# Moving early pooling and gate work between GpSimd, ScalarE and VectorE, and two products ahead, in a pooled-attention and mixture-of-experts kernel

## The chip, the cores and the metric

The kernel runs on one core of one Trainium2 chip. The metric is the time of one execution on the device in microseconds (us). A core has a matrix engine (TensorE, PE in the profile; its weight loads are listed as PEld) and three engines for elementwise work: VectorE (DVE), ScalarE (ACT) and GpSimd (POOL). The DMA issues named here come from SyncE (SP) or GpSimd. PE and its accumulators meet in PSUM; everything else is in SBUF. Each engine runs its instructions in the order in which the kernel issues them to it.

## The reference

All tensors are float32. An attention over keys and values that are averaged in groups of eight is followed by a mixture of experts in which each token goes to one expert:

```python
B, H, S, D = 8, 8, 576, 64            # q, k, v
k_p = k.reshape(B, H, 72, 8, D).mean(axis=3)
v_p = v.reshape(B, H, 72, 8, D).mean(axis=3)
scores = scale * q @ k_p.T            # 576 x 72 for each batch and head
attn = exp(scores - max); attn /= sum(attn) + 1e-9
x = (attn @ v_p) laid out as 4608 tokens x 512

N, D, E, F = 4608, 512, 8, 1024
logits = x @ w_gate + modality_bias[modality_id]
e_idx = argmax(logits); gate = softmax(logits)[e_idx]
out[token] = gate * (relu(x @ w1[e_idx]) @ w2[e_idx])
```

The inputs q, k and w_gate are drawn eight times as large as their base draw, so that the softmax is not flat.

## The kernel before, in words

**Stages.** The attention with its routing fills about the first 170 us; the products of the expert stage (lines 193, 196, 1314 of the profile) take most of the rest. The change lies in the attention.

**Tiles and steps.** A tile is 128 tokens with all eight heads. A batch of 576 tokens has four tiles of 128 and 64 tokens over; the 64 tokens of two batches make one mixed tile. So a pair of batches has nine tiles, and `steps` lists five steps for it: two tiles, two tiles, the mixed tile, two tiles, two tiles. There are 20 steps. Steps 0 and 1 are batch 0 (tiles 0 to 3), step 2 is mixed tile 4, which needs the keys and values of batches 0 and 1, steps 3 and 4 are batch 1 (tiles 5 to 8), step 5 is the first of batch 2. Each step handles its heads in two halves, written (n,0) and (n,1).

**What a step does.** The helpers are named after their engine:

- `q_pe`/`q_act` (L555, L561): PE transposes the queries into a PSUM slot, ScalarE copies them out to `qt`.
- `s_pe` (L574 mixed, L580): the scores, from `qt` and the keys `kt`. `s_dve` (L587, L590) takes the row maximum and subtracts it; `s_act` (L602, L603) takes the exponent.
- `t_pe`/`t_act` (L609, L614) transpose a tile's weights and copy them to `pt`; `t4_pe`/`t4_act` (L621, L628) do it for the eight pooled keys of every head beyond the first 64.
- `a_pe` (L644, L648): the tile's products with the values, into the one `av` buffer of PSUM. `x_dve` (L667 to L677) divides by the sums and writes the tokens to `xb`; it is what frees `av` for the next tile.

**Keys and values.** The keys of a batch come as four chunks of 128 partitions x 512 elements and a smaller one. Averaging folds the 512 elements to 64. `fold` does it on GpSimd with three adds (L330 to L332), `reduce8` on VectorE with one reduction (L335). In `pool_k` and `pool_v`, conditions on the batch number choose who folds which chunk; `pool_k_rest` and `pool_v_rest` fold one chunk (number 3) later, on VectorE. `kp` has one buffer, `vp` two. `k_operand` (PE transposes, then two ScalarE copies, L383 and L384, to `kt`) runs in two parts, for chunks 0 to 2 and for the rest. `v_operand` copies the folded values with masks to `vw` and `v4` and transposes them for the gate (pv, L422 and L423; the copy out of PSUM to `vt`, L427 and L428). `v_gate` multiplies them by `w_gate` on PE, so that the logits come out of the same products as the tokens. The gate product lands in a corner of a score bank, three blocks wide. ScalarE writes two of them with masks to `vw`; the third goes by a ScalarE copy `vg4` (L444) and a GpSimd product with the mask `m4b` (L445) to `v4`.

**PSUM slots.** q_pe, k_operand, v_operand and t_pe share two slots of the tag `tr`; the scores have two buffers, `av` has one.

**Order.** All order is written by hand. The main loop runs over the steps n; in it the helpers stand in one sequence, and lists of functions (`hook_0` to `hook_3`, `hook_q`) add the work for the next batches at five places. For the steps that matter here they hold:

- step 1: `hook_0` pool_v(1), pool_k(2); `hook_q` k_operand(1, 0); `hook_2` pool_v_rest(1), k_operand(1, 1)
- step 2: `hook_1` v_operand(1); `hook_2` v_gate(1)
- step 3: `hook_0` pool_v(2); `hook_1` k_operand(2, 0); `hook_2` pool_v_rest(2); `hook_q` k_operand(2, 1)
- step 4: `hook_0` pool_k(3); `hook_1` v_operand(2); `hook_2` v_gate(2)

In step n the tiles of step n-1 are finished: `old[0]` behind `hook_1`, `old[1]` near the end, behind `hook_2`. In the lines below, `old` is that pair, and `has`, `nxt` tell whether step n and step n+1 exist:

```python
            run(hook_1, n)
            if old:
                a_pe(old[0])
            if has:
                s_dve(n, 1)
```

**Routing.** When both batches of a pair are through, their routing operations (L726 to L786, nearly all on VectorE) go into a list `drip`, from which `gap()` takes operations between the others. The first group is worked off in steps 6 and 7, 62 to 73 us.

**Loads.** SP issues the loads in an order of their own, by step (`step_loads`). In step 0 it issues k(2), the rest of k(2), v(2), its rest, and k(3); in step 1 q(2), v(3), the rest of k(3), the modality numbers and k(4). A whole k, v or q of a batch is 1 MB.

Of the kernel before, what the change touches and what calls it, by code (L numbers as in the profile page):

```python
# [9 lines left out]
F32 = mybir.dt.float32  # L10
# [5 lines left out]
ALU = mybir.AluOpType  # L16
# [6 lines left out]
P = 128  # L23
# [10 lines left out]
def kernel(  # L34
# [12 lines left out]
    nc = tc.nc  # L47
    ctx.enter_context(tc.manual_schedule(engines=ENGINES))
    B, H, S, HD = q.shape
    NTOK, D = out.shape  # L50
    E, _, FF = w1.shape
    POOL = 8
    SPL = S // POOL
    NPAIR = H // 2
# [163 lines left out]
    with ExitStack() as actx:  # L218
        ap = actx.enter_context(tc.tile_pool(name="ap", bufs=1))
# [5 lines left out]
        kraw, k4raw, vraw, v4raw, qpure, qmix = {}, {}, {}, {}, {}, {}  # L225
# [100 lines left out]
        kps, vps, vts = {}, {}, {}  # L326

        def fold(t, out):

            nc.gpsimd.tensor_add(t[..., 0:256], t[..., 0:256], t[..., 256:512])  # L330
            nc.gpsimd.tensor_add(t[..., 0:128], t[..., 0:128], t[..., 128:256])
            nc.gpsimd.tensor_add(out, t[..., 0:64], t[..., 64:128])  # L332

        def reduce8(t, out):
            nc.vector.tensor_reduce(out, t.rearrange("p (u d) -> p d u", u=POOL), axis=AX.X, op=ALU.add)  # L335
# [4 lines left out]
        def pool_k(b, parts=(0, 1)):  # L340
            if b not in kps:
                kps[b] = (ap.tile([P, NCH, HD], F32, tag="kp", bufs=1, name=f"kp_{b}"),
                          ap.tile([64, HD], F32, tag="kp4", bufs=1, name=f"kp4_{b}"))
            kp, kp4 = kps[b]
            t, t4 = kraw[b], k4raw[b]
            for i in parts:
                cs = K_PART[i]
                if b == 0:
                    for c in cs:
                        reduce8(t[:, c, :], kp[:, c, :])  # L350
                    if i == 1:
                        reduce8(t4, kp4)
                else:
                    for c in range(cs[0], cs[-1] + 1, 2):
                        m = min(c + 2, cs[-1] + 1)
                        if b == 1 and c == 2:
                            reduce8(t[:, c, :], kp[:, c, :])
                        elif b > 1 or c < 2:
                            fold(t[:, c:m], kp[:, c:m])
                    if i == 1:  # L360
                        fold(t4, kp4)
# [24 lines left out]
        def pool_v(b):  # L386
            vp = ap.tile([P, NPAIR, HD], F32, tag="vp", bufs=2, name=f"vp_{b}")
            vp4 = ap.tile([P, HD], F32, tag="vp4", bufs=2, name=f"vp4_{b}")
            t, t4 = vraw[b], v4raw[b]
            if b == 0:  # L390
                fold(t4, vp4)
            fold(t[:, 0:2], vp[:, 0:2])
            if b > 2:
                fold(t[:, 2:4], vp[:, 2:4])
            elif b:
                fold(t[:, 2], vp[:, 2])
            else:
                fold(t[:, 2], vp[:, 2])
                reduce8(t[:, 3, :], vp[:, 3, :])
            if b:  # L400
                fold(t4, vp4)
            vps[b] = (vp, vp4)

        def pool_k_rest(b):
            reduce8(kraw[b][:, 3, :], kps[b][0][:, 3, :])

        def pool_v_rest(b):
            reduce8(vraw[b][:, 3, :], vps[b][0][:, 3, :])

        m4b = m_4.rearrange("p (j o) -> p j o", o=1)  # L410

# [18 lines left out]
        def v_gate(b):  # L430
            vt, vt4 = vts[b]
            dw, d4 = vw[b % NB], v4[b % NB]
            if b:
                pg = spare[1][:, 1, 4 * SPL:4 * SPL + 12 * E].rearrange("p (u x) -> p u x", u=3)
            else:
                pg = ps_tr.tile([P, 3, 4 * E], F32, tag="tr", name=f"pg_{b}")
            for u in range(2):
                nc.tensor.matmul(pg[:, u, :], vt[:, u, :], wgb[:, u].rearrange("p g x -> p (g x)"), start=True, stop=True)
            nc.tensor.matmul(pg[:, 2, :], vt4, wg[0:64, 1::2, :], start=True, stop=True)
            pgv = pg[:, 0:2, :].rearrange("p u (g a e) -> p (u g) a e", g=2, a=2)  # L440
            nc.scalar.activation(dw[:, :, 0, HD:HD + E], pgv[:, :, 0, :], AF.Copy, scale=m_a)
            nc.scalar.activation(dw[:, :, 1, HD:HD + E], pgv[:, :, 1, :], AF.Copy, scale=m_b)
            vg4 = ap.tile([P, NPAIR, E], F32, tag="vg4", bufs=1, name=f"vg4_{b}")
            nc.scalar.copy(vg4, pg[:, 2, :].rearrange("p (j e) -> p j e", j=NPAIR))  # L444
            nc.gpsimd.tensor_tensor(d4[:, :, HD:HD + E], vg4, m4b.to_broadcast([P, NPAIR, E]), op=ALU.mult)  # L445


        bias_all = ap.tile([P, NT, E], F32, name="bias_all")
# [74 lines left out]
        def gap(n=2):  # L523

            for _ in range(n):
                if drip and drip[0] not in held:
                    drip.pop(0)()
# [31 lines left out]
        def q_act(n, w):  # L559
            pq = pqs.pop((n, w))  # L560
            nc.scalar.copy(qts[n, w][:, 0:2 * len(steps[n][2]), :], pq)  # L561
# [21 lines left out]
        def s_dve(n, w):  # L583
            nh = 2 * len(steps[n][2])
            scv = scs.pop((n, w))[:, :, 0:nh * SPL].rearrange("p u (h s) -> p u h s", s=SPL)
            mx = ap.tile([P, 2, 4], F32, tag="mx", bufs=2, name=f"mx_{n}_{w}")[:, :, 0:nh]
            nc.vector.reduce_max(mx, scv, axis=AX.X)  # L587
            gap()
            sb = ap.tile([P, 2, 4 * SPL], F32, tag="sb", bufs=2, name=f"sb_{n}_{w}")
            nc.vector.tensor_tensor(sb[:, :, 0:nh * SPL].rearrange("p u (h s) -> p u h s", s=SPL), scv,  # L590
                                    mx.rearrange("p u (h o) -> p u h o", o=1).to_broadcast([P, 2, nh, SPL]), op=ALU.subtract)
            scs[n, w] = sb
# [19 lines left out]
        def t_act(t):  # L612
            pt = ap.tile([P, NPAIR, P], F32, tag="pt", bufs=2, name=f"pt_{t}")
            nc.scalar.copy(pt, pts[t])  # L614
            pts[t] = pt
# [265 lines left out]
        for g in range(len(GROUPS) - 1):  # L881
            n = s1_of[2 * g + 1] + 2
# [65 lines left out]
        def run(hook, n):  # L948
            for fn in hook.get(n, ()):
                fn()  # L950
# [6 lines left out]
        for n in range(N + 1):  # L957
            has, nxt, nxt2 = n < N, n + 1 < N, n + 2 < N
            old = steps[n - 1][2] if n else ()
            two = len(old) > 1  # L960
            ahead = two and has and steps[n][1] is None
            loads(n)
            run(hook_0, n)
            if old:
                t_pe(old[0])
                t_act(old[0])
                if has:
                    s_act(n, 0)
            if has:
                s_pe(n, 1)  # L970
            if due:
                release()
            if old:
                t4_pe(n - 1)
                t4_act(n - 1)
            if n == N:
                run(hook_3, N - 1)
            if ahead:
                t_pe(old[1])
                t_act(old[1])  # L980
            run(hook_1, n)
            if old:
                a_pe(old[0])
            if has:
                s_dve(n, 1)
            if n == 1:
                pool_k_rest(1)
            finish()
            if n == 0:
                q_pe(1, 0)  # L990
                q_act(1, 0)
                v_operand(0)
            if two and not ahead:
                t_pe(old[1])
                t_act(old[1])
            if n == 1 or n == 2:
                q_pe(n + 1, 0)
                q_act(n + 1, 0)
            if nxt:
                q_pe(n + 1, 1)  # L1000
            run(hook_q, n)
            if old:
                x_dve(old[0])
            gap(2)
            if nxt and n:
                q_act(n + 1, 1)
            if has:
                s_act(n, 1)
            if n == 0:
                q_act(n + 1, 1)  # L1010
            if nxt:
                s_pe(n + 1, 0)
            if nxt2 and n > 1:
                q_pe(n + 2, 0)
                q_act(n + 2, 0)
            if nxt:
                s_dve(n + 1, 0)
            if n == 0:
                v_gate(0)
                pool_k(1)  # L1020
            run(hook_2, n)
            finish()
            due = bool(drip) and drip[0] in held
            if two:
                a_pe(old[1])
            if two:
                x_dve(old[1])
            gap(2)
            if n != N - 1:
                run(hook_3, n)  # L1030
            finish()
# [13 lines left out]
    op = [[ps_op.tile([P, 512], F32, name=f"op{i}_{z}") for z in range(2)] for i in range(2)]  # L1045
# [533 lines left out]
```

## Time and profile before

| | |
|---|---|
| time, median of 3 runs | 593.8 us (593.5 to 594.74) |
| the profiled execution | 596.24 us, of which span 594.5 us |
| granted TensorE clock | 0.999 |
| PE busy | 574.1 us, 97% of the span |
| PE weight loads | 499.5 us, 84% |
| DVE busy | 371.9 us, 63% |
| ACT busy | 275.1 us, 46% |
| POOL busy | 192.0 us, 32% |
| DMA | 92.60 MB, mean 156 GB/s |

The span is the time from the first to the last instruction of the profiled execution; the time of that execution has 1.74 us around it. The shares are averages over the whole span, and the stages differ: GpSimd is busy 32% on average, but 60% to over 90% of each of the first eight of the page's 40 equal slices of the span, 119 us, in which it folds keys and values. In lists of instructions, each row has the start in us, the length in us, the engine, the line, the operation, output and input, the tile's shape and the count of like instructions in a row; in brackets stands the idle time of the engine before it and what ended it.

### The profile page before, as it was taken

How to read it: one execution, taken by the hardware profiler on the slowest of the kernel's cores; microseconds unless marked ns; L12 is line 12 of the kernel's file. 1: busy time of each engine (PE TensorE's matmuls, PEld its weight loads, DVE VectorE, ACT ScalarE, POOL GpSimd, SP SyncE). 2: the span in 40 equal slices, each digit the busy share in tenths (PEclk: the TensorE clock that was granted, in tenths of full speed). 3: DMA queues.
4: the chain of work that ended last, by engine and by line, in shares of the span. 5: the costliest groups of instructions: out<-in, count | busy, mean ns of one | idle time of the engine just before them, and what ended most of it. 6: DMA issues, size and time to landing. Idle time of an engine off the chain costs nothing.

```text
span 594.5 us, 12358 instructions
## 1 busy us (share of the span) xinstructions
PE 574.1 (97%) x3539; PEld 499.5 (84%) x3539; DVE 371.9 (63%) x941; ACT 275.1 (46%) x653; POOL 192.0 (32%) x300
## 2 busy tenths in 40 slices
PE   5899999999999999999999999999999999999995
PEld 4789889888898888888888888888888888888994
DVE  5757888789966775566555457855455487465311
ACT  2657667788552233334333337533333474334210
POOL 6689987755000142112102203212102203202101
PEclk9999999999999999999999999999999999999999
DMA  8999979995311752232232377232335742332001
GB/s 247 288 333 265 352 236 309 308 292 177 110 56 39 262 189 85 94 104 92 101 96 92 106 231 233 91 105 92 106 93 179 238 153 79 115 103 87 37 2 55
DMA packets 83426, 92.60 MB, mean 156 GB/s; under 512 B 17871, under 2 KB 58319, under 8 KB 83344
## 3 DMA queue, kind: packets, MB, share of 16 engines
q1 hardware_dynamic: 77424, 72.24, 39.0%
q0 software_dynamic: 5920, 19.44, 9.9%
q8 instruction: 30, 0.49, 0.3%
q14 instruction: 52, 0.43, 0.2%
HBM read 123.06 MB, written 27.58 MB: 253 GB/s over the span
## 4 chain that ended last, share of the span: by engine, by line
PE 78%; DVE 9%; DMA 8%; ACT 2%; issue 1%; POOL 1%; SPq 1%; POOLq 0%; DVEq 0%; ACTq 0%
PE op L1314 32%; PE hp L193 19%; PE hp L196 10%; DMA k<-in_k_dram 5%; PE av L644 4%; PE hp L183 3%; PE sc L580 2%; PE av L648 2%; PE ph L183 1%; PE pp L609 1%; DMA mod<-in_moe_modality_id_dram 1%; DMA xs<-xb 1%; DVE mx L587 1%; DMA out_dram<-obw,slw 1%; PE pq L555 1%
## 5 line engine op out<-in xcount | busy, mean ns | idle before, releaser
L1314 PE MATMUL op<-hl,hh 128*128 128x512 f32 x512 | 161.1, 396 | 0.0
L193 PE MATMUL hp<-xhl,hl 128*128 128x512 f32 x512 | 137.1, 389 | 0.0
L1290 POOL DMA_INDIRECT out_dram<-ob,sidx x34 | 36.6, 1075 | 263.6 <-DVEq L1319 178.6
L193 PEld LDWEIGHTS hp<-xhl,hl 128*128 128x128 f32 x512 | 96.0, 188 | 20.6
L198 ACT COPY ht<-hp 128x256 f32<-128x256 f32 x128 | 47.8, 373 | 130.8 <-PE hp L196 129.8
L199 DVE TENSOR_TENSOR ht<-ht,hp 128x256 f32<-128x256 f32 x128 | 53.7, 419 | 85.7 <-ACT ht L198 84.2
L1314 PE MATMUL op<-hl,hlo 128*128 128x512 f32 x256 | 99.8, 390 | 0.0
L1314 PEld LDWEIGHTS op<-hl,hh 128*128 128x128 f32 x512 | 88.0, 190 | 11.3
L202 DVE SCALAR_TENSOR_TENSOR hlo<-ht,hh 128x256 fp32r<-128x256 f32 x128 | 55.1, 431 | 55.6 <-ACTq L1319 45.4
L196 PEld LDWEIGHTS hp<-xhl,hl 128*128 128x128 f32 x512 | 78.3, 189 | 10.1
L200 ACT ACTIVATE hh<-ht 128x256 fp32r<-128x256 f32 x128 | 53.7, 420 | 67.5 <-DVE ht L199 67.5
L196 PE MATMUL hp<-xhl,hl 128*128 128x256 f32 x512 | 81.3, 281 | 0.0
L1314 PEld LDWEIGHTS op<-hl,hlo 128*128 128x128 f32 x256 | 48.1, 188 | 11.2 <-DVE hlo L202 0.3
L644 PE MATMUL av<-vw,pt 128*128 128x146 f32 (+1 forms) x320 | 49.5, 293 | 1.7 <-DVE xb L677 1.6
L144 POOL DMA_INDIRECT xg<-xs,gidx x36 | 38.6, 1073 | 31.6 <-DVE sidx L815 16.4
L644 PEld LDWEIGHTS av<-vw,pt 128*128 128x128 f32 (+1 forms) x320 | 39.7, 180 | 3.8 <-DVE xb L677 1.4
L580 PE MATMUL sc<-kt,qt 128*128 128x144 f32 x256 | 37.4, 289 | 1.2 <-ACT qt L561 1.0
L580 PEld LDWEIGHTS sc<-kt,qt 128*128 128x128 f32 x256 | 33.1, 190 | 2.2 <-ACT qt L561 0.9
L587 DVE TENSOR_REDUCE mx<-sc 128x8 f32<-128x576 f32 (+1 forms) x40 | 27.6, 691 | 8.1 <-PE sc L580 6.0
L648 PE MATMUL av<-vw,pt 128*128 128x146 f32 (+1 forms) x160 | 30.6, 289 | 0.2 <-POOL vw L445 0.2
L590 DVE TENSOR_TENSOR sb<-sc,mx 128x576 f32<-128x576 f32 (+1 forms) x40 | 27.7, 692 | 2.4 <-DVE mx L587 0.5
L141 DVE TENSOR_TENSOR hl<-raw,hl 128x1024 fp32r<-128x1024 f32 x24 | 29.0, 1217 | 0.0
(277 smaller groups left out, 825.5 us busy)
## 6 DMA issues: line engine op xcount, KB each, us to landing
raw<-in_moe_w_dram SPq DMA_DIRECT2D x288, 256.0 KB
xs<-xb SPq DMA_DIRECT2D x16, 528.0 KB
scr<-xg SPq DMA_DIRECT2D x29, 256.0 KB
k<-in_k_dram SPq DMA_DIRECT2D x7, 1024.0 KB
v<-in_v_dram SPq DMA_DIRECT2D x7, 1024.0 KB
q<-in_q_dram SPq DMA_DIRECT2D x7, 1024.0 KB
y<-scr SPq DMA_DIRECT2D x108, 64.0 KB
v<-in_v_dram SPq DMA_DIRECT2D x16, 128.0 KB
```

Of the source, the lines that this page charges most:

```text
L144: nc.gpsimd.indirect_dma_start(out=x, out_offset=None, in_=xs[0:rows, :], in_offset=IndirectOffsetOnAxis(idx[:, col:col + 1].bitcast(U32), 0),
L193: nc.tensor.matmul(ph, hl[f][:, 0, d * P:(d + 1) * P], ab[:, d, :, 0:SLOT], start=(d == 0), stop=False)
L196: nc.tensor.matmul(ph[:, 0:SLOT], hl[f][:, 1, d * P:(d + 1) * P], ab[:, d, 0, 0:SLOT], start=False, stop=(d == ND - 1))
L198: nc.scalar.copy(t, ph[:, SLOT:2 * SLOT])
L199: nc.vector.tensor_add(t, t, ph[:, 0:SLOT])
L200: nc.scalar.activation(hh, t, AF.Relu)
L202: nc.vector.scalar_tensor_tensor(hlo, t, 0.0, hh.bitcast(F32), op0=ALU.max, op1=ALU.subtract)
L580: nc.tensor.matmul(dst, qt[:, i, :], kt[b % NB][:, :, h * SPL:(h + 1) * SPL], start=True, stop=True)
L644: nc.tensor.matmul(av[hs, u, 2 * VC * gg:2 * VC * (gg + 1)], pt[:, c, hs], vw[y][:, c].rearrange("p a x -> p (a x)"), start=(gg == 0), sto ...
L648: nc.tensor.matmul(dst4[hs], pt4[:, hs], v4[y][:, 2 * u:2 * u + 2, :], start=False, stop=True)
L1290: nc.gpsimd.indirect_dma_start(out=out[:, :], out_offset=IndirectOffsetOnAxis(idx.bitcast(U32), 0), in_=ob, in_offset=None, bounds_check=N ...
L1314: nc.tensor.matmul(ot, l[:, ts_], hl[f][:, w, D:2 * D], start=(f == 0 and n == 0), stop=(f == NF - 1 and n == 2))
```

## The change

- **Folds.** Chunks 2 and 3 of the keys of batch 2 and chunk 2 of the values of batch 1 are no longer folded by GpSimd (three chunks). VectorE does them: the value chunk and the last chunk of k(1) in step 1 behind `s_act(1,1)`, the chunks of k(2) in step 2 behind `s_act(2,1)` and behind `s_dve(3,0)`. The fold of the last chunk of k(1) stood ahead of the x_dve of tile 0 before and stands behind it now.
- **Products ahead.** In step 1 the products and the x_dve of tile 1 go ahead of the first scores of the mixed step (`s_pe(2,0)`); they stood behind `hook_2`. In step 2 the products of tile 2 go ahead of `hook_1`, that is of v_operand(1).
- **Gate product.** In `v_gate`, for every batch, the third block is multiplied by the mask by VectorE, straight out of PSUM into `v4`; the ScalarE copy and the buffer `vg4` are gone, and so is the GpSimd product.

```diff
@@ pool_k
                         if b == 1 and c == 2:
                             reduce8(t[:, c, :], kp[:, c, :])
-                        elif b > 1 or c < 2:
+                        elif b > 2 or c < 2:
                             fold(t[:, c:m], kp[:, c:m])
@@ pool_v
             if b > 2:
                 fold(t[:, 2:4], vp[:, 2:4])
-            elif b:
+            elif b == 2:
                 fold(t[:, 2], vp[:, 2])
-            else:
+            elif b == 0:
                 fold(t[:, 2], vp[:, 2])
                 reduce8(t[:, 3, :], vp[:, 3, :])
...
-        def pool_k_rest(b):
-            reduce8(kraw[b][:, 3, :], kps[b][0][:, 3, :])
-
-        def pool_v_rest(b):
-            reduce8(vraw[b][:, 3, :], vps[b][0][:, 3, :])
+        def pool_k_rest(b, c=3):
+            reduce8(kraw[b][:, c, :], kps[b][0][:, c, :])
+
+        def pool_v_rest(b, c=3):
+            reduce8(vraw[b][:, c, :], vps[b][0][:, c, :])
@@ v_gate
-            vg4 = ap.tile([P, NPAIR, E], F32, tag="vg4", bufs=1, name=f"vg4_{b}")
-            nc.scalar.copy(vg4, pg[:, 2, :].rearrange("p (j e) -> p j e", j=NPAIR))
-            nc.gpsimd.tensor_tensor(d4[:, :, HD:HD + E], vg4, m4b.to_broadcast([P, NPAIR, E]), op=ALU.mult)
+            nc.vector.tensor_tensor(d4[:, :, HD:HD + E], pg[:, 2, :].rearrange("p (j e) -> p j e", j=NPAIR),
+                                    m4b.to_broadcast([P, NPAIR, E]), op=ALU.mult)
@@ main loop
+            if n == 2:
+                a_pe(old[0])
             run(hook_1, n)
-            if old:
+            if old and n != 2:
                 a_pe(old[0])
             if has:
                 s_dve(n, 1)
-            if n == 1:
-                pool_k_rest(1)
...
+            if n == 1:
+                pool_k_rest(1)
+                pool_v_rest(1, 2)
+                a_pe(old[1])
+                x_dve(old[1])
+            if n == 2:
+                pool_k_rest(2, 2)
             if nxt:
                 s_pe(n + 1, 0)
...
             if nxt:
                 s_dve(n + 1, 0)
+            if n == 2:
+                pool_k_rest(2)
...
             run(hook_2, n)
...
-            if two:
+            if two and n != 1:
                 a_pe(old[1])
-            if two:
                 x_dve(old[1])
```

## The prediction

> **What bounds the kernel now.** I read the page's busy shares first, then the windows, then who TensorE (PE) waits for, then the timelines of the attention stage, engine by engine. The page and the windows (columns: busy us with instruction counts of PE, PEld, DVE, ACT, POOL; granted clock; DMA share; GB/s) show where PE is not full:
>
> ```profile
> PE 574.1 (97%) x3539; PEld 499.5 (84%) x3539; DVE 371.9 (63%) x941; ACT 275.1 (46%) x653; POOL 192.0 (32%) x300
> 20.00:30.00 10.00, 8.88 (x66) 7.26 (x65) 7.92 (x16) 6.12 (x18) 7.69 (x12) 1.00 1.08 306
> 40.00:45.00 5.00, 4.83 (x46) 3.88 (x45) 3.29 (x9) 2.76 (x9) 4.68 (x9) 1.00 1.09 356
> 50.00:62.00 12.00, 12.00 (x100) 11.64 (x99) 8.61 (x23) 7.65 (x21) 11.14 (x20) 1.00 1.06 342
> 62.00:73.00 11.00, 10.03 (x82) 8.46 (x81) 10.01 (x31) 8.37 (x26) 10.04 (x20) 1.00 1.06 341
> 170.00:580.00 410.00, 409.94 (x2183) 351.60 (x2182) 235.31 (x574) 160.50 (x348) 76.55 (x77) 1.00 0.36 117
> ```
>
> From 170 to 580 us PE idles 0.06 us: a microsecond won or lost before 170 reaches the end unchanged. So the question is what PE waits for in steps 1 to 4 of the attention loop (20 to 50 us), where the diff moves work, and whether what is won there lasts. The waits of PE, 20 to 80 us (total, times, longest):
>
> ```profile
> PE av L644 <- DVE xb L677: 0.9, 2, 0.6
> PE sc L574 <- ACT kt L384: 0.7, 1, 0.7
> PE pv L422 <- DVE vp L335: 0.5, 1, 0.5
> PE pv L423 <- POOL vp L332: 0.4, 1, 0.4
> PE av L648 <- POOL vw L445: 0.2, 1, 0.2
> ```
>
> The last four lie between 25 and 49 us and the change touches three of them; the first lies in the first routing group (68 to 73 us). PE's timeline there (start, length, x count, idle before), and last a row of VectorE's:
>
> ```profile
> 25.80 0.46 PE L574 MATMUL sc<-kt,qt 128*64 128x144 f32 x2
> 26.92 0.70 PE L574 MATMUL sc<-kt,qt 128*64 128x144 f32 x6 [0.66 <-ACT kt L384]
> 27.96 0.77 PE L644 MATMUL av<-vw,pt 128*128 128x146 f32 x4
> 29.56 0.60 PE L609 MATMUL pp<-ident,pe 128*128 128x128 f32 x4
> 32.12 0.30 PE L423 MATMUL pv<-ident,vp 128*64 128x128 f32 x1 [0.41 <-POOL vp L332]
> 33.76 1.04 PE L555 MATMUL pq<-ident,q 128*128 128x128 f32 x8
> 42.08 0.34 PE L648 MATMUL av<-vw,pt 128*64 128x146 f32 x1 [0.17 <-POOL vw L445]
> 23.83 1.04 DVE L335 TENSOR_REDUCE kp<-k 128x64 f32<-128x512 f32 x1
> ```
>
> **The change, part by part.**
>
> *Tile 1's products (a_pe(1)) ahead of the mixed step's scores.* They take 27.96 to 29.56 = 1.60 us. Placed at 25.80 they fill the wait for ScalarE's key copy, which ends the idle at 26.92: about 0.9 us regained. They need the av buffer free of x_dve(0); the fold of k(1)'s last chunk, which stood ahead of x_dve(0) and takes 1.04 us (last row above), now stands behind it, so VectorE (DVE) reads av sooner and I charge nothing; were it late all the same, the price is at most that 1.04. The cover then lacks elsewhere (estimates from laying the rows out in the new order): the last key chunk's copies, hidden by those products before, now hold s_pe(2,1) some 0.2 us, and s_dve(2,0), queued behind x_dve(1), holds the small transpose L621 another 0.2.
>
> *Tile 2's products ahead of v_operand(1).* They cover POOL's last v4 fold, wait 0.41 us. The transposes pv then stand directly before q_pe(3,1), which needs their PSUM slot: 0.2 us back.
>
> *Three chunk folds from POOL to DVE.* The prices:
>
> ```profile
> 30.40 0.73 POOL L330 TENSOR_TENSOR v<-v 128x256 f32<-128x256 f32 x1
> 31.75 0.32 POOL L332 TENSOR_TENSOR vp<-v 128x64 f32<-128x64 f32 x1
> 28.60 1.05 DVE L335 TENSOR_REDUCE vp<-v 128x64 f32<-128x512 f32 x1
> 33.96 0.17 DVE L667 TENSOR_SCALAR r<-av 128x8 f32<-128x8 f32 x1 [1.95 <-PE av L648]
> ```
>
> One chunk is 1.67 us on POOL (30.40 to 32.07, three adds) and 1.05 on DVE: POOL loses 5.0 us, DVE gains 3.2, all before 38 us. There DVE idles between tiles, 1.95 us ahead of the x_dve at 33.96, and the fold of k(2) stands ahead of scores that come later than its data. I cost the DVE part at nothing; without that cover it is 1.05 us each. No DMA, SP or POOL issue is moved past another; POOL's later folds only come forward.
>
> *The gate product on DVE, eight times.*
>
> ```profile
> L444 ACT COPY vg<-sc x7: 184/185/192, 37.9 to 147.5; 128x32 f32<-128x32 f32 x7
> L445 POOL TENSOR_TENSOR vw<-vg,m x8: 233/240/249, 21.2 to 149.2; 128x32 f32<-128x32 f32 x8
> 67.78 0.22 DVE L673 TENSOR_TENSOR lg<-av,r 128x64 f32<-128x64 f32 x1
>   ACT xb L669: 3.4, 7
> ```
>
> ACT loses 8 x 0.185, POOL 8 x 0.24 and its waits for ACT. DVE gains eight products of 32 columns. L673, twice as wide and also from PSUM, takes 0.22 but its successor starts 0.13 later, so 0.15 each (bounds 0.13 and 0.22). A new wait comes with it: VectorE's L673 waits for ScalarE's L669 on the same PSUM tile, 3.4 us in 7 (the last row), though both only read. So the product will wait for ScalarE's two reads of the same bank; behind it on DVE stands x_dve of the next tile. By the timelines ScalarE is through first, or DVE would idle anyhow, except in step 16, where both about cancel. The Trainium skill, "PSUM — Partial Sum Buffer", section "PSUM bank collisions raise a hardware error", says that two engines may not read one bank at once; the 3.4 us agree, and by it the wait belongs there.
> The product costs time only where DVE sets PE's pace: once, in the first routing group, 0.15. For mixed tile 4, step 3, it also removes the wait at 42.08, 0.2 us and up to 0.6 of disorder around it.
>
> Sum up to q_pe(5,0): 0.9 + 0.4 + 0.6 - 0.6 = 1.3; bounds 0.9 (nothing at tile 4 and all new waits) and 2.1 (ScalarE's q copies and the key copies also come early).
>
> **Where the gain stops.** q_pe(5,0) reads q(2), whose load is far back in a full queue (the DMA share is 1.06 to 1.09 up to 45 us):
>
> ```profile
> 10.68 9.61 DMA k<-in_k_dram
> 20.31 13.43 DMA k<-in_k_dram
> 28.89 1.28 SPq L269 DMA_DIRECT2D q<-in_q_dram  x1
> 45.18 0.60 PE L555 MATMUL pq<-ident,q 128*128 128x128 f32 x4
> 45.61 0.85 PE L609 MATMUL pp<-ident,pe 128*128 128x128 f32 x4
> 47.39 0.27 PE L422 MATMUL pv<-ident,vp 128*128 128x128 f32 x1
> 48.12 0.30 PE L422 MATMUL pv<-ident,vp 128*128 128x128 f32 x1 [0.45 <-DVE vp L335]
> 50.30 0.60 PE L555 MATMUL pq<-ident,q 128*128 128x128 f32 x4
> 46.02 0.60 ACT L561 COPY qt<-pq 128x512 f32<-128x512 f32 x1
> 49.48 0.26 ACT L427 COPY vt<-pv 64x128 f32<-64x128 f32 x1
> ```
>
> k(2), of the same 1 MB, landed 13.43 us after its issue (row of the chain). q(2), issued at 28.89 behind as full a queue, lands then at 42.3 or later, and before 45.18, since PE read it then without a wait. The queue was growing (k(1) had landed 9.61 us after its issue), so I take the upper end, 44.9. PE now comes there at 45.18 - 1.3 = 43.9 (43.1 at best) and waits until 44.95, whatever was won before.
> But the wait lets DVE and ScalarE catch up. PE's stall for the value fold (47.50 to 48.12, 0.62) goes, as does 0.25 in L609 (0.85 against 0.60 elsewhere). PE alone would reach the next L555 at 44.95 + (50.30 - 45.18) - 0.87 = 49.2. ScalarE's chain runs without a break from L561 at 46.02 to L427's end at 49.74, 3.72 us; starting at 45.57 it frees the PSUM slot at 49.3. So L555 starts at 49.3 instead of 50.30: a gain of 1.0 (0.9, or up to the 2.1 if q(2) came early).
> From 50 to 62 PE is busy all 12.00 us, so nothing stops it and 1.0 remains.
>
> **The first routing group, 63 to 73 us,** is a DVE chain that PE waits for (0.9 in 2).
>
> ```profile
> 65.31 1.40 DVE L728 TENSOR_TENSOR bias_all<-bias_all,sc 128x288 f32<-128x288 f32 x1
> 69.66 0.66 DVE L739 TENSOR_TENSOR oh<-w,m 128x72 bf16<-128x72 f32 x1
> 71.10 0.44 DVE L590 TENSOR_TENSOR sb<-sc,mx 128x288 f32<-128x288 f32 x1
> ```
>
> L728 takes 1.40 where L590 does the same width out of PSUM in 0.44, and POOL is busy 10.04 of these 11 us: VectorE's operations on two SBUF tensors are held up there, 0.96 in L728, some 0.4 in L739 (L673 does 64 columns in 0.22). With POOL's folds earlier, these meet other POOL operations. Bounds: all 1.4 us gone, or each of the six such operations held for a long POOL add, about 1 us each. Nearest are the rows as they stand; since three of the six met no delay, I charge 0.2.
> The Trainium skill, "SBUF — State Buffer", section "SBUF: two separate sides", calls this an exclusive lock that the loser waits out; the 1.40 agrees. By that rule the reduces (one source) and the PSUM product never wait for it, as L335's 1.05 beside a busy POOL shows, and only these routing operations could turn the gain round.
>
> **Sum:** 1.0 - 0.15 - 0.2 = 0.65, with ScalarE's shorter queue in step 16 some 0.05 more: 0.7 us. The profiled execution took 596.24 us with a span of 594.5 (1.74 around it), 2.4 above the median of 593.8; its terms carry over as differences: 594.5 - 0.7 = 593.8 span, and 593.8 - 0.7 = 593.1 us as the median. About 0.2% (1.2 us) is what a measurement of this kernel can tell from no change.
>
> **The rivals.**
> *R1, q(2) does not hold PE.* It lands near 42.3; then the early gain stays whole, 2.1, less 0.15 and 0.2: 592.0 us. For it: the lower bound from k(2). Against: the queue is longer by then. Chance 0.18.
> *R2, slower: VectorE behind POOL in the first routing group.* If the six SBUF operations meet POOL's long adds, the chain grows by more than the 1.0 won; it decides at 1.0 us extra, and is measurable above 2.2. Three more hits like L728's 0.96 make 2.9 - 1.0 + 0.15 = 2.0: 595.8 us. For it: three of the six were lucky. Against: PE has slack of its own after each. Chance 0.15.
> *R3, nothing comes through:* DVE, in order, waits for k(2) (landed at 33.73) ahead of the scores and PE reaches q(2) no earlier than before: 593.8 us. Against: 1.3 us of reserve. Chance 0.1.
> *Forecast:* 0.57, its own range 592.4 to 593.9.
>
> Range 591.7 to 595.1: R1, R3 and the milder half of R2. Faster by over 0.2% (below 592.6): R1 and a fifth of the forecast, 0.3. Within: the rest of the forecast, R3 and a small part of R2, 0.6. Slower: R2's measurable part, 0.1.
>
> **What would show it.** Right: no wait of L574 for L384 and none of L423 or L648 for POOL; a new idle before L555 near 44 us, ended by the DMA of q, 1 to 2 us; L422's wait for L335 gone; PE at the same instruction 1.0 us earlier at 50 and 0.5 to 1.0 at 74; L728 and L739 of other lengths. Wrong: no idle before q_pe(5,0) (R1), or PE waiting longer for xb L677 near 73 (R2), or PE waiting for DVE at 28 to 34 us (R3).

## The result: slower by 1.1%, and where the time went

The changed kernel takes 600.49 us (median of 6 runs, 598.0 to 605.22) against 594.27 us of the kernel before (median of 6, 593.5 to 595.79). The ratio is 1.0109, 95% interval [1.0082, 1.0137]. The forecast was 593.1 us, range 591.7 to 595.1. The profiled execution took 601.39 us, span 599.7 us, at a mean granted clock of 0.994.

The page of the changed kernel starts with the busy times:

```profile
PE 576.2 (96%) x3539; PEld 502.4 (84%) x3539; DVE 383.4 (64%) x952; ACT 275.7 (46%) x645; POOL 186.2 (31%) x283
```

Against before, GpSimd has 5.8 us less to do and VectorE 11.5 us more. The three folds and eight products that moved are only some 4.6 us of that (3 x 1.05 us and 8 x 0.18 us). The other 7 us of VectorE are the first thing that asks for an explanation.

The windows of the changed kernel, then those of before (busy us of PE, PEld, DVE, ACT, POOL; granted clock; DMA share; GB/s):

```profile
45.00:62.00 17.00, 17.00 (x139) 16.64 (x140) 12.64 (x31) 12.46 (x35) 15.65 (x28) 1.00 1.04 326
62.00:75.00 13.00, 10.79 (x78) 9.55 (x77) 10.75 (x33) 5.96 (x18) 12.06 (x21) 0.87 1.05 353
88.00:100.00 12.00, 9.95 (x79) 9.09 (x78) 11.33 (x33) 6.74 (x18) 8.26 (x11) 1.00 1.01 326
100.00:118.00 18.00, 16.09 (x134) 14.66 (x133) 14.70 (x41) 11.90 (x35) 13.62 (x22) 1.00 0.85 282
118.00:150.00 32.00, 30.05 (x259) 28.00 (x258) 26.61 (x72) 26.20 (x65) 12.31 (x21) 0.95 0.61 197
```

```profile
62.00:75.00 13.00, 12.03 (x98) 10.46 (x98) 11.40 (x35) 8.59 (x26) 11.96 (x23) 1.00 1.05 349
88.00:100.00 12.00, 12.00 (x100) 11.67 (x99) 10.10 (x34) 8.79 (x24) 7.54 (x13) 1.00 0.92 280
100.00:118.00 18.00, 18.00 (x156) 16.18 (x156) 14.35 (x43) 13.54 (x38) 15.55 (x25) 1.00 1.00 329
```

Up to 62 us the changed kernel is the better one. Then PE idles more than before: 2.21 us instead of 0.97 between 62 and 75 us, 2.05 and 1.91 us instead of none in the next two windows shown, and 1.95 instead of 0.75 us between 118 and 150 us. In two windows the granted clock is 0.87 and 0.95. PE's timeline of the changed kernel, the rows with a wait that matter here:

```profile
42.52 0.63 PE L554 MATMUL pq<-ident,q 128*128 128x128 f32 x4 [0.32 <-DMA q<-in_q_dram]
62.73 0.44 PE L554 MATMUL pq<-ident,qm 128*128 128x128 f32 x2
69.50 0.71 PE L573 MATMUL sc<-kt,qt 128*64 128x144 f32 x8 [2.14 <-DVE vw L443]
92.65 0.77 PE L643 MATMUL av<-vw,pt 128*128 128x146 f32 x4 [1.34 <-DVE xb L676]
95.35 1.25 PE L579 MATMUL sc<-kt,qt 128*128 128x144 f32 x8 [0.50 <-DVE vw L443]
113.10 0.71 PE L573 MATMUL sc<-kt,qt 128*64 128x144 f32 x8 [1.91 <-DVE vw L443]
134.68 0.77 PE L643 MATMUL av<-vw,pt 128*128 128x146 f32 x4 [1.37 <-DVE xb L676]
171.90 0.66 PE L608 MATMUL pp<-ident,pe 128*128 128x128 f32 x4 [0.54 <-DVE h L187]
```

The same places before (the last row is the same matmul as the last one above):

```profile
25.02 0.44 PE L555 MATMUL pq<-ident,qm 128*128 128x128 f32 x2 [0.46 <-ACT pt L614]
65.85 0.44 PE L555 MATMUL pq<-ident,qm 128*128 128x128 f32 x2
165.44 0.66 PE L609 MATMUL pp<-ident,pe 128*128 128x128 f32 x4 [0.53 <-DVE h L187]
```

At the first of these rows the changed kernel stands at 24.06 us, 0.96 ahead; 0.82 of that it had already at the first load of q that PE waits for (13.22 against 14.04 us), ahead of the change. At 62.73 it is 3.12 ahead, so it has won 2.16 us. At 171.90 it is 6.46 behind. Between the two lie 9.6 us lost. The waits shown for VectorE, and two small ones of 0.20 us (VectorE) and 0.37 us (ScalarE), make 7.83 us, where before had 1.59 (0.30, 0.57 and 0.72, all for VectorE): 6.2 more. The clock takes 13 x 0.13 + 32 x 0.05 = 3.3 us. Together that is 9.5. Behind 172 us the changed kernel's span is 1.3 us shorter than that of before. All other kernels of this study are shorter there too, by 0.6 to 1.4 us (the kernel with the old gate product: 1.1), so it is not the gate product's.

L443 is the new gate product on VectorE. The scores wait for it because it reads a corner of the score bank that the next scores overwrite; before, ScalarE's copy (L444) gave that bank back. That suggested one theory (**the bank**: VectorE's product stands late in its queue and holds the score buffer). The waits for xb do not fit it. The other theory came from GpSimd. Rows of GpSimd before, and then of the changed kernel at the same place:

```profile
88.00 0.61 POOL L417 TENSOR_TENSOR vw<-vp,m 128x256 f32<-128x256 f32 x1
92.59 0.24 POOL L445 TENSOR_TENSOR vw<-vg,m 128x32 f32<-128x32 f32 x1 [3.98 <-ACT vg L444]
92.79 1.27 POOL L330 TENSOR_TENSOR v<-v 128x512 f32<-128x512 f32 x1
```

```profile
87.35 0.61 POOL L417 TENSOR_TENSOR vw<-vp,m 128x256 f32<-128x256 f32 x1
87.92 1.26 POOL L330 TENSOR_TENSOR v<-v 128x512 f32<-128x512 f32 x1
90.49 1.26 POOL L330 TENSOR_TENSOR v<-v 128x512 f32<-128x512 f32 x1
```

Before, GpSimd stood still for 3.98 us in front of its gate product, since ScalarE's copy came late. With the product gone it goes straight on to the next folds. In just these microseconds VectorE works off routing operations. Rows of VectorE, before and after (arow, the nine one-hot rows of the first group; they come at 85 to 91 us, behind the 62 to 73 us given for that group above):

```profile
87.76 1.06 DVE L786 TENSOR_SCALAR arow<-iota_b,rkf 128x128 bf16<-128x128 bf16 x2
89.49 0.24 DVE L786 TENSOR_SCALAR arow<-iota_b,rkf 128x128 bf16<-128x128 bf16 x1
```

```profile
87.11 2.29 DVE L785 TENSOR_SCALAR arow<-iota_b,rkf 128x128 bf16<-128x128 bf16 x2
90.61 1.19 DVE L785 TENSOR_SCALAR arow<-iota_b,rkf 128x128 bf16<-128x128 bf16 x1
```

An operation of 0.24 us takes 1.19 us beside a GpSimd add (90.61 to 91.80 us; the add runs from 90.49 to 91.75). That is the second theory (**the pause**: the wait that the change removed had kept GpSimd's folds away from VectorE's routing). A third was that the folds and the new order cost the time themselves.

### The profile page after: what moved, and what is told of

It reads as the page before. It is cut to its first block, busy times and chain, and to the rows that moved or that the text cites. A ratio compares the mean times of both kernels' runs of the same rounds, so it can differ in the third digit from the quotient of the medians.

```text
span 599.7 us, 12342 instructions
## 1 busy us (share of the span) xinstructions
PE 576.2 (96%) x3539; PEld 502.4 (84%) x3539; DVE 383.4 (64%) x952; ACT 275.7 (46%) x645; POOL 186.2 (31%) x283
## 4 chain that ended last, share of the span: by engine, by line
PE 73%; DVE 11%; DMA 7%; POOL 3%; issue 3%; ACT 1%; SPq 0%; POOLq 0%; DVEq 0%; ACTq 0%
PE op L1321 32%; PE hp L193 19%; PE hp L196 10%; DMA k<-in_k_dram 6%; PE hp L183 3%; PE av L643 3%; PE sc L579 2%; DVE sb L589 1%; PE ph L183 1%; PE av L647 1%; DVE arow L785 1%; DVE mx L586 1%; POOL k L330 1%; DVE hl L141 1%; DVE xb L676 1%
## 5 line engine op out<-in xcount | busy, mean ns | idle before, releaser
L643 PE MATMUL av<-vw,pt 128*128 128x146 f32 (+1 forms) x320 | 50.6, 298 | 3.0 <-DVE xb L676 2.7
L643 PEld LDWEIGHTS av<-vw,pt 128*128 128x128 f32 (+1 forms) x320 | 41.0, 185 | 4.9 <-DVE xb L676 3.5
L647 PE MATMUL av<-vw,pt 128*128 128x146 f32 (+1 forms) x160 | 31.0, 297 | 0.4 <-ACT pt L627 0.4
```

What stands on the lines that cost most here:

```text
L643: nc.tensor.matmul(av[hs, u, 2 * VC * gg:2 * VC * (gg + 1)], pt[:, c, hs], vw[y][:, c].rearrange("p a x -> p (a x)"), start=(gg == 0), sto ...
L647: nc.tensor.matmul(dst4[hs], pt4[:, hs], v4[y][:, 2 * u:2 * u + 2, :], start=False, stop=True)
```

## The experiments

Each ratio is against executions of the kernel before that were taken together with that kernel's; their medians lie between 594.31 and 595.13 us.

**The old gate product on the changed kernel, and the new one alone on the kernel before.** The first keeps folds and order and puts the copy and the GpSimd multiply back; the second is the opposite.

```diff
-nc.vector.tensor_tensor(d4[...], pg[:, 2, :]..., m4b..., op=ALU.mult)
+nc.scalar.copy(vg4, pg[:, 2, :]...)
+nc.gpsimd.tensor_tensor(d4[...], vg4, m4b..., op=ALU.mult)
```

> The changed kernel with the old gate product (ScalarE copy out of PSUM, GpSimd multiply); folds and reordered products stay. Bank theory (VectorE's gate product frees the score bank late, PE waits 4.75 us for it in four places) and pause theory (GpSimd lost its waits for ScalarE's copy, 11.5 us in 4, and its folds now run against VectorE's routing operations) both put the whole loss on the gate product: 592 us, the 2.2 us by which the trace after is ahead at 62 us being kept. Third theory, the folds and the new order cost the time themselves: 597 us or more.

> The kernel before with the gate product on VectorE and nothing else of the change. Bank theory: PE waits for that product again in the mixed steps, some 4 to 5 us and what the clock loses behind them, 598 to 602 us. Pause theory: GpSimd's pauses are gone too, waits of the value products for xb near 92 and 134 us, 2.7 us, 597 us. Third theory (folds and order): 594 us, as before.

Measured: 593.37 us with the old product (592 was expected by the first two theories), ratio 0.9981 [0.9965, 0.9997]; 600.38 us with the new product alone, ratio 1.0121 [1.0091, 1.015]. The third theory falls: folds and order win about 1.1 us, and the gate product alone costs 5.9. The second time does not separate the other two theories; by itself it lies where the bank theory had put it. Its trace is of the fastest of six executions, 597.38 us: from 23.53 us, 1.49 ahead of before, PE falls 1.35 behind at the matmul that stands at 165.44 before. So the trace shows 2.8 us of the loss, with 3.6 us of waits for xb and 1.9 for the product; where the slower executions (up to 605.42 us) lose the rest, no trace shows.

**ScalarE gives the bank back, GpSimd has no pause.** Two forms on the changed kernel: ScalarE copies the block out and VectorE multiplies the copy; or ScalarE does the product itself.

```diff
+nc.scalar.copy(vg4, pg[:, 2, :]...)
-nc.vector.tensor_tensor(d4[...], pg[:, 2, :]..., m4b..., op=ALU.mult)
+nc.vector.tensor_tensor(d4[...], vg4, m4b..., op=ALU.mult)
```

```diff
-nc.vector.tensor_tensor(d4[...], pg[:, 2, :]..., m4b..., op=ALU.mult)
+for j in range(NPAIR):
+    nc.scalar.activation(d4[:, j, HD:HD + E], pg[:, 2, j * E:(j + 1) * E], AF.Copy, scale=m_4[:, j:j + 1])
```

> The changed kernel, but ScalarE copies the third gate block out of PSUM as before and VectorE multiplies the copy: ScalarE frees the score bank, GpSimd still has no pause. Bank theory: no wait of the scores for the gate product, 592 to 594 us. Pause theory: the waits for xb near 92 and 134 us stay (2.7 us) and routing operations stay long, 595 us or more; the new product reads two SBUF tensors and may be held up itself.

> The changed kernel, but ScalarE does the third gate product itself, in four instructions with the mask as scale, straight out of PSUM: the score bank is freed by ScalarE, VectorE has no gate product, and GpSimd still has no pause. Bank theory alone: 593.5 us. Pause theory: the waits of the value products for xb near 92 and 134 us stay, 1.3 us each, and routing operations stay long, 596 to 598 us (600.5 less the 4 us of waits for the bank that the paused kernel had left).

Measured: 601.65 us, ratio 1.013 [1.0105, 1.0155], and 601.84 us, ratio 1.0108 [1.0078, 1.0137]. Neither gains anything on the changed kernel, not even the 4 us expected of the second, which lies above what either theory gave. In the first form the product, now with two SBUF inputs, is itself held in part: its eight instances take 0.19 to 1.09 us, against 0.17 to 0.19 out of PSUM. PE's waits of the second form:

```profile
PE av L643 <- DVE xb L676: 3.6, 4, 1.4
PE sc L620 <- DVE sb L589: 2.2, 3, 1.2
PE sc L573 <- ACT vw L444: 1.5, 2, 0.9
```

The bank is free earlier, and PE meets the same late VectorE a little further on, at the scores' subtraction (sb) and at xb. So here the bank was the place where PE met the delay, not its cause.

**GpSimd gets its pause back.** On the changed kernel, VectorE's product stays; on the second form above, ScalarE's product stays. Each time GpSimd copies one column that ScalarE has written, and nobody uses the copy (in the second, the column is one of `d4`).

```diff
+pz = ap.tile([P, 1], F32, tag="pz", bufs=1, name=f"pz_{b}")
+nc.gpsimd.tensor_copy(pz, dw[:, 0, 1, HD:HD + 1])
```

> The changed kernel plus one GpSimd copy of one column that ScalarE's second gate product has written, at the place of the old GpSimd multiply, so that GpSimd waits for ScalarE there again; the gate product stays on VectorE. Pause theory: the long operations of VectorE and the waits for xb near 92 and 134 us go, and with them most of the waits for the bank: 592 to 595 us. Bank theory: the waits of the scores for the gate product stay, 598 us.

> The same with one GpSimd copy of one column of ScalarE's last gate product, so that GpSimd waits there: both causes are taken away at once. If they are the two causes, the time is that of the kernel with the old gate product, 593 to 594 us, and below the kernel without the pause by about 3 us. If the pause does nothing here, both are the same.

Measured: 597.33 us, ratio 1.0048 [1.0031, 1.0066], and 595.56 us, ratio 1.001 [0.9993, 1.0028]. The added work, 8 copies of some 0.18 us, makes the kernels 3.2 and 6.3 us faster. Both times lie above what was expected if the pause is the cause (592 to 595 us, and 593 to 594 for the second, which takes both causes away); the first is nearer to the bank theory's 598. The groups of VectorE from 60 to 180 us show how (busy, mean ns of one), in this order: before; the changed kernel; the changed kernel with the pause; ScalarE's product without and with the pause:

```profile
L786 DVE TENSOR_SCALAR arow<-iota_b,rkf 128x128 bf16<-128x128 bf16 x27 | 8.6, 347 | 0.0
```

```profile
L785 DVE TENSOR_SCALAR arow<-iota_b,rkf 128x128 bf16<-128x128 bf16 x27 | 13.6, 533 | 0.0
```

```profile
L787 DVE TENSOR_SCALAR arow<-iota_b,rkf 128x128 bf16<-128x128 bf16 x27 | 8.6, 347 | 0.0
```

```profile
L785 DVE TENSOR_SCALAR arow<-iota_b,rkf 128x128 bf16<-128x128 bf16 x27 | 13.6, 532 | 0.0
```

```profile
L787 DVE TENSOR_SCALAR arow<-iota_b,rkf 128x128 bf16<-128x128 bf16 x27 | 8.7, 348 | 0.0
```

The 5.0 us come and go with the pause alone, whoever does the product. With the pause the waits for xb near 92 and 134 us are gone too, but for 0.28 us on the second kernel. What stays on the first of the two is the bank's wait in the mixed steps, 4.3 us with a third one of 0.21 us, and it is what its time had too much:

```profile
72.44 0.71 PE L575 MATMUL sc<-kt,qt 128*64 128x144 f32 x8 [3.00 <-DVE vw L443]
112.62 0.71 PE L575 MATMUL sc<-kt,qt 128*64 128x144 f32 x8 [1.09 <-DVE vw L443]
```

On the second, PE waits 1.6 us in two mixed steps for ScalarE's products, where the old copy on the changed kernel cost 0.47. Whether that is why its ratio stands above the 0.9981 of that kernel was not tried, and the two intervals overlap.

**A pause in the first routing group as well.** There GpSimd reached its gate product too late to wait for anything, in the kernel before and also where it had the added copy. Folding the last parts of k(4) and k(6) behind the product instead of ahead of it lets GpSimd arrive early. This went onto the kernel with the old product, onto the changed kernel with the one-column copy, and onto the kernel before.

```diff
-at(hook_0, m, lambda b=b: pool_k(b + 2))
+at(hook_0, m, lambda b=b: pool_k(b + 2, (0,) if b in (2, 4) else (0, 1)))
 at(hook_2, m, lambda b=b: v_gate(b + 1))
+if b in (2, 4):
+    at(hook_2, m, lambda b=b: pool_k(b + 2, (1,)))
```

> The changed kernel with the old gate product, and the last chunk and the rest of k(4) and k(6) folded on GpSimd behind the gate product of batch 3 and 5 instead of ahead of it, so that GpSimd's pause for ScalarE falls into the first routing group. Pause theory: the operations of VectorE at 66 to 69 us are held less, PE's waits there (0.47 + 0.53 + 0.62 us) shrink, 592 to 593 us. Otherwise 593.4 us; slower if the later folds hold PE.

> The changed kernel, its gate product on VectorE, with the one-column GpSimd copy that waits for ScalarE and with the last chunk and the rest of k(4) and k(6) folded behind it: GpSimd pauses in the first routing group too. Pause theory: VectorE is not held, its gate product comes in time and PE's waits for the bank shrink from 4.3 us to under 1.5: 593.3 us. Bank theory (the product is late in VectorE's queue whatever GpSimd does): the waits stay near 4 us, 597 us.

> The kernel before with only that move of k(4)'s and k(6)'s last folds. Pause theory: the wait of 0.57 us for xb near 73 us shrinks, and up to 1 us may be given back near 84 us: 593.6 to 594.8 us. Were the pause worth nothing without the rest, the time would be that of before within 0.1%.

Measured: 592.77 us, ratio 0.9956 [0.9938, 0.9974]; 592.32 us, ratio 0.998 [0.9965, 0.9995]; 594.81 us, ratio 1.001 [0.9999, 1.0021]. The second is the one that decides. It has VectorE's gate product and VectorE gives back the bank, as in the changed kernel. The first routing group in the changed kernel, VectorE's rows and the GpSimd add beside them:

```profile
67.41 1.58 DVE L756 TENSOR_SCALAR sm<-sm 128x9 f32<-128x9 f32 x1
68.90 0.44 DVE L589 TENSOR_TENSOR sb<-sc,mx 128x288 f32<-128x288 f32 x1
69.27 0.17 DVE L443 TENSOR_TENSOR vw<-sc,m 128x32 f32<-128x32 f32 x1
67.70 1.25 POOL L330 TENSOR_TENSOR v<-v 128x512 f32<-128x512 f32 x1
```

and in this one, with GpSimd's row of the pause last:

```profile
66.36 0.17 DVE L758 TENSOR_SCALAR sm<-sm 128x9 f32<-128x9 f32 x1
66.44 0.45 DVE L591 TENSOR_TENSOR sb<-sc,mx 128x288 f32<-128x288 f32 x1
66.84 0.19 DVE L443 TENSOR_TENSOR vw<-sc,m 128x32 f32<-128x32 f32 x1
66.87 0.19 POOL L446 COPY pz<-vw 128x1 f32<-128x1 f32 x1 [2.24 <-ACT vw L442]
```

An operation on nine columns falls from 1.58 to 0.17 us (0.33 in the kernel before), the product comes in time, and PE's waits for it shrink from 4.7 us to 0.2. The bank theory, by which they should have stayed near 4, is gone as a cause of its own. On the kernel before the move wins nothing: PE's wait of 0.57 us near 73 us becomes 0.30, and a wait at 86 us grows from 0.48 to 1.21, so it is given back, as was feared.

**Only the small rest behind the product** (of k(4) and k(6), with the old product).

```diff
-    fold(t4, kp4)                      # ahead, in pool_k
+at(hook_2, m, lambda b=b: fold(k4raw[b + 2], kps[b + 2][1]))   # behind v_gate
```

> The changed kernel with the old gate product, and only the small rest of k(4) and k(6) (three adds, 1.6 us) behind the gate product, the last chunk ahead: a shorter pause in the first routing group (from 67 us), less folding in the second half of it. Between the kernel with the old gate product and the one with both moved: 592.3 to 593.3 us; better than the latter if PE's wait at 84 us (1.53 us there) falls back to 0.5.

Measured: 592.56 us, ratio 0.9971 [0.9953, 0.9989]. PE's wait for a VectorE subtraction at 84 us, 1.53 us with the full move, fell back to 0.48, as hoped, while 0.34 and 0.40 us of waits in the group returned. Its interval overlaps that of the full move, so the two cannot be told apart, nor either from the kernel with the old product alone. All three are faster than both kernels of the case.

**The order alone** (kernel before with the two products ahead and the last fold of k(1) behind the x_dve of tile 0; the three chunks and the gate product as before).

```diff
+if n == 2:
+    a_pe(old[0])
 run(hook_1, n)
...
+if n == 1:
+    pool_k_rest(1)
+    a_pe(old[1])
+    x_dve(old[1])
```

> The kernel before with the two products put ahead and the late fold of k(1) behind the x_dve of tile 0; the three chunks stay on GpSimd and the old gate product stays. By the prediction's terms the order gives 0.9 + 0.4 - 0.6 = 0.7 us before the load of q(2) and the folds add 0.4 to 0.6 more through the value fold and tile 4: 593.7 us. If the folds carry the gain, 594.4; if the order carries all of it, 593.3.

Measured: 594.54 us, ratio 0.9987 [0.997, 1.0004]. The interval cannot separate that from zero, but PE's timeline can: corrected for its earlier start (23.93 against 25.02 us) it is 0.96 us ahead at the value fold (46.07 against 48.12). The kernel with folds and order is 2.17 ahead there in the same way (24.64; 45.57).

## Why the prediction was wrong

**Right: folds and order.** The forecast's first part, 1.0 us from these two, is near what the kernel with the old gate product shows: 1.1 us, with an interval from 0.2 to 2.1. The agreement is in part luck, since the load that was to cap the gain at 1.0 did not: that kernel is 2.17 us ahead at 45.57 us and still 1.70 at the matmul that stands at 165.44 before, each corrected for its start. PE's waits for the key copy, for GpSimd's value fold and for L445 went as foretold; that of L422 for VectorE's fold shrank from 0.45 to 0.20 us and did not vanish.

**Mis-sized: the load of q(2).** It was to land at 44.9 us, 16.1 behind its issue, and hold PE 1 to 2 us. In the changed kernel PE waited 0.32 us, at 42.5; in the two kernels with ScalarE's product 1.05 and 2.11 us. The rows with that wait start at 42.52, 44.28 and 45.59 us, 15.5, 15.4 and 16.6 us behind the issue. So the time from issue to landing was nearly right; what moves is the issue, 27.04, 28.88 and 29.01 us here and 25.82 to 29.25 over all runs, and the prediction had taken the 28.89 of one trace for a constant. PE's early gain was larger, too: 2.0 us where 1.3 was expected (it is free for q(2) at 42.20 against 45.18, less the 0.96 at the start). The gain at 62 us was 2.16 us, the size of the rival R1.

**Wrong, and it decided: "POOL 8 x 0.24 and its waits for ACT".** The prediction booked the removed waits of GpSimd as work that ScalarE and GpSimd lose. The list of waits of before has the row (total, times, longest):

```profile
POOL vw L445 <- ACT vg L444: 11.5, 4, 4.0
```

The prediction did not ask what those waits keep apart. "The product costs time only where DVE sets PE's pace: once, in the first routing group, 0.15" was off by a factor of about 40: the product costs 5.9 us by itself. With GpSimd's waits put back, and one more in the first routing group, the same product on VectorE costs nothing that these runs can tell: 592.32 us, and 592.77 with the old product in the same order of folds.

**Wrong: which operations can be held.** The rival R2 had the mechanism, VectorE held up beside GpSimd, at 0.15. But it counted "six such operations", those with two SBUF sources in the first group. Several of the 27 arow operations and the one on nine columns, with one tensor and a scalar, are held just so (0.24 to 1.19, 0.17 to 1.58 us); the second group has them as well, so the cost does not end with the first. The Trainium skill, "SBUF — State Buffer", section "SBUF: two separate sides", names VectorE's two-port modes beside operations with two SBUF inputs, and the prediction had used only the second half of that sentence. That one-tensor operations can be held agrees with the 1.19 and 1.58 us; in which mode they ran, no run here shows.

**Wrong: who waits for a moved read.** For the new product the prediction asked what stands behind it on VectorE, not who reuses the PSUM bank that it reads. That made the score buffer's release a matter of VectorE's queue. It costs PE only while VectorE is late: 4.7 us in the changed kernel, 4.3 with the pause missing in the first routing group, 0.2 with both pauses.

**Not thought of: the clock.** Windows of one us in the changed kernel: five after the wait of 2.14 us, one after the wait of 1.91, and four after that of 1.37 (columns as in the windows above; the granted clock stands third from the end):

```profile
70.00:71.00 1.00, 1.00 (x10) 0.81 (x6) 1.00 (x4) 0.42 (x2) 1.00 (x2) 0.73 1.04 363
71.00:72.00 1.00, 1.00 (x6) 1.00 (x6) 0.97 (x3) 0.69 (x2) 0.92 (x2) 0.50 1.06 416
72.00:73.00 1.00, 1.00 (x6) 1.00 (x6) 0.40 (x1) 0.00 (x0) 0.92 (x3) 0.50 1.03 396
73.00:74.00 1.00, 1.00 (x6) 1.00 (x6) 0.00 (x0) 0.00 (x0) 0.92 (x2) 0.56 1.05 366
74.00:75.00 1.00, 1.00 (x11) 1.00 (x10) 0.82 (x4) 0.40 (x1) 0.92 (x3) 1.00 1.10 358
114.00:115.00 1.00, 1.00 (x10) 0.97 (x9) 0.82 (x2) 0.98 (x5) 0.86 (x2) 1.00 0.35 37
135.00:136.00 1.00, 1.00 (x8) 1.00 (x7) 0.90 (x2) 0.00 (x0) 0.92 (x3) 0.66 0.00 0
136.00:137.00 1.00, 1.00 (x6) 1.00 (x6) 0.25 (x2) 0.00 (x0) 0.65 (x2) 0.50 0.00 0
137.00:138.00 1.00, 1.00 (x6) 0.99 (x6) 0.37 (x2) 0.37 (x1) 0.00 (x0) 0.50 0.00 0
138.00:139.00 1.00, 1.00 (x8) 1.00 (x7) 0.23 (x1) 0.88 (x3) 0.00 (x0) 0.63 0.00 0
```

Twice the clock is halved for 3.42 us (0.54 + 1 + 1 + 0.88, and 0.68 + 1 + 1 + 0.74, worked out from the rows' means), 1.7 us of work each time. That is the 3.3 us of the account above. It explains the spread of the executions in part: the two at a mean clock of 1.000 took 598.0 and 598.32 us, the three at 0.994 took 601.39, 602.08 and 605.22 us. What parts the last three is open.

## What to carry to other kernels

Before a wait is removed from an engine that is not the bottleneck, look at what that engine does next and whom it can hold up there; an idle time can be what keeps two engines apart. When the reader of a PSUM tile moves to another engine, the tile's next writer now waits for that engine's whole queue. When a suspected wait is taken away and PE merely waits at the next place, look for the engine that is late and ask why its operations got longer: the same instruction with another mean duration in the groups names the cause.

## What the runs showed of the hardware that was not expected

- An operation of VectorE on nine columns took 1.58 us instead of 0.17 while GpSimd ran an add of 1.25 us. The score operations out of PSUM did not change: the 40 reductions have a mean of 691 ns before and 692 ns in the changed kernel, the 40 subtractions 692 and 693 ns.
- The clock fell to half after a wait of 1.37 us and not after one of 1.91 us, each time for about 3.4 us. The Trainium skill, "TensorE: Matmul & The Clock Gate", section "What's actually happening", tells of a free-running window of 3.4 us after which an idle array is halved; the length agrees and a window that runs by itself would fit the chance character, but here a stretch with far less idle time than a window, 1.37 us, was enough. What decides it was not tried.
